# Zero products in TensorE's planned pauses, and a fourth head pair moved by products

## The chip, the cores and the metric

The kernel runs on one core of a Trainium2 chip. The metric is the device time of one execution in microseconds, and a kernel is told by the median of its runs. The time before is 1008.89 us, the median of 3 runs (1008.83 to 1009.3).

## What is computed

```python
# 4 batches, 8 heads, 768 steps, head width 48
for t in range(S):
    state = alpha[:, :, t, :, None] * state + k_t (outer) v_t     # per batch and head
    y[:, :, t] = q_t @ state
x = y as 3072 tokens x 384                                        # fp32
x = ((x @ w_a) * (x @ w_b)) @ w_out            # first network, 384 -> 1536 -> 384
h = x @ w_in
out = (max(h, 0) + alpha2 * min(h, 0)) @ w_out2 # second network, 384 -> 2048 -> 384
```

The weights of both networks arrive as 8-byte floats; q, k, v and alpha are fp32.

## The kernel before

**Chunks and blocks.** The recurrence is cut into 24 chunks of 128 steps of one batch. Four chunks, one of each batch, make a block of 512 tokens, so there are six blocks. A chunk loads its decays (tile La), keys (Lk), queries (Lq) and values (v) over the one DMA queue (SP). VectorE makes the running products of the decays backwards and forwards by two scans (R, L303, and La in place, L313), multiplies the keys by the one (L317) and the queries by the other (L321). TensorE transposes the keys (kps, L360), makes the step-by-step scores (A, L377), the new state (dS, L402), and the output y from the masked scores As (L412) and, from the second block on, from the kept state Z (L422). ScalarE and VectorE split y into a high and a low part (tile x, L464 and L468). Most tiles of a chunk have two buffers (`Ring(2)`): the load of chunk g+2 waits for the last reader of chunk g.

**The fourth pair.** Eight heads of width 48 are four pairs, each padded to two halves of 64 rows. The networks want 384 rows in three groups of 128, so the rows of the fourth pair have to go into the padding of the first three. In block 0 (`start`) TensorE makes the fourth pair first, ScalarE copies it (y3, L449), and a product with a constant 0/1 matrix `shift` adds it to each of the other three (L454). In blocks 1 to 5 six DMAs move the rows inside the tile x (L486).

**Weights.** A unit is 256 columns of one weight matrix; the first network has 18 (a0, b0, o0 to a5, b5, o5), the second 16. `conv` turns a unit of 8-byte floats into a high and a low fp32 part: ScalarE takes the magnitude (L195), VectorE does sign (L203), a clamp from below (L199), main (L208), power (L212) and rest (L216), ScalarE makes the high part (L221), VectorE subtracts it (L224) and adds the rest (L228).

**The networks.** A step of the first network is two up products (pa, pb, nine matmuls each), a copy and a multiplication (a_sb, L627, L630), a split (gh, gl, L526, L530) and, two steps later, nine down matmuls into three accumulators (acc). Each product is three passes (L503, L504, L506). `SEGMENTS` orders the steps: units 0 and 1 for block 0 (four steps), the same for block 1, then units 2 and 3 for either, and so on; then the second network.

**The order of the work.** Nothing is ordered by hand. All operations go into a `Graph` with an engine, a planned duration, a priority (`key`) and their dependences; `Graph.run` plays them through with these durations and writes each engine's instructions in the planned order. At run time each engine works through its own list in that order and waits where it must. Chunks of block 0 have the lowest keys, then the units and chunks by due time. Three PSUM tiles (`ps_mm`) take the up products. Before, `up` takes them by a ring in order of creation (`mring`). `a_sb` has two buffers, handed out by `bring = Ring(2)`.

At the start VectorE clears a tile and TensorE multiplies it eight times (`WARM`, L149).

Of the kernel before, what the change touches and what calls it, by code (L numbers as in the profile page):

```python
# [21 lines left out]
P = 128  # L22
# [9 lines left out]
WARM = 8  # L32
# [6 lines left out]
URGENT = 40000  # L39


class Op:
    __slots__ = ("eng", "dur", "fn", "key", "lat", "need", "users", "soft", "ready", "end", "n")


class Graph:
# [3 lines left out]
    def __init__(self):  # L50
        self.ops = []

    def add(self, eng, dur, fn, key, deps=(), lat=0, after=()):
        o = Op()
        o.eng, o.dur, o.fn, o.key, o.lat = eng, dur, fn, key, lat
        o.users, o.soft, o.ready, o.end, o.need, o.n = [], [], 0, None, 0, len(self.ops)
        for d in {x for x in deps if x is not None}:
            d.users.append(o)
            o.need += 1
        for d in {x for x in after if x is not None}:  # L60
            d.soft.append(o)
            o.need += 1
        self.ops.append(o)
        return o

    def run(self):
        free, ready = {}, {}
        for o in self.ops:
            free.setdefault(o.eng, 0)
            ready.setdefault(o.eng, [])  # L70
            if not o.need:
                ready[o.eng].append(o)
        for _ in range(len(self.ops)):
            best = None
            for e, l in ready.items():
                if l:
                    t = max(free[e], min(o.ready for o in l))
                    if best is None or t < best[0]:
                        best = (t, min((o for o in l if o.ready <= t), key=lambda o: (o.key, o.n)))
# [12 lines left out]

# [19 lines left out]
def body(tc, akq, v, w_a, w_b, w_o1, w_in, w_o2, beta, out):  # L112
# [13 lines left out]
    with ExitStack() as ctx:  # L126
# [31 lines left out]
        )  # L158

        shift = wpool.tile([P, KT, P], F32, name="shift", tag="s1")  # L160
# [8 lines left out]
        G = Graph()  # L169
# [12 lines left out]
        cring = Ring(2)  # L182

        def conv(src, tag, name, key, wait, sink, early=15000):
# [7 lines left out]
            def magnitude():  # L192
                b["c1"] = cpool.tile([P, UC], F32, name="c1", tag="c1")
                b["c2"] = cpool.tile([P, UC], F32, name="c2", tag="c2")
                nc.scalar.activation(out=b["c1"], in_=b["raw"].bitcast(F32)[:, 1::2], func=ACTF.Abs,  # L195
                                     scale=65536.0)

            def floor():
                nc.vector.tensor_scalar(out=b["c1"], in0=b["c1"], scalar1=2.0, scalar2=None,  # L199
                                        op0=ALU.max)  # L200
# [33 lines left out]
            y = G.add("DVE", 550, sign, key, [m])  # L234
            x = G.add("DVE", 550, floor, key, [m, y])
# [7 lines left out]
            return ld, x  # L243

# [4 lines left out]
        for u in range(NU1):  # L249
            for nm, src in (("a", w_a), ("b", w_b), ("o", w_o1)):  # L250
                x = nm, u
                slot_of[x] = len(slot_of)
                uses[x] = []

                def sink(r, x=x):
                    units[x] = as_unit(r, 2 if x[0] == "o" else KT)

                _, done[x] = conv(src[u], f"w{slot_of[x]}", f"{nm}{u}", due[x] - 20000, (), sink)
# [6 lines left out]
        before = {"scan": None, "y3": None}  # L265
# [3 lines left out]
        def chunk(g):  # L269
            s = st[g]  # L270
            n, c = divmod(g, BC)
            start, end = n == 0, n == NB - 1
# [7 lines left out]
            def load(nm, lo, hi):  # L280
                def f():
                    s[nm] = tp.tile([P, hi - lo], F32, name=f"L{nm}", tag=f"L{nm}")
                    nc.sync.dma_start(s[nm], akq[g, :, lo:hi])
                return f
# [5 lines left out]
            kT = lambda: s["k"].rearrange("p (j t) -> p j t", j=NJ)  # L290
            qT = lambda: s["q"].rearrange("p (j t) -> p j t", j=NJ)
            rings = {nm: lrings[nm] for nm in "akq"}
            w = {nm: rings[nm].take() for nm in "akq"}
            use = {nm: rings[nm].use for nm in "akq"}
            la = A("SP", 800, load("a", 0, NA), w["a"], 14000, 2500)
            lk = A("SP", 800, load("k", NA, NA + NC), w["k"], 13900, 2500, [la])
            lq = A("SP", 800, load("q", NA + NC, NA + 2 * NC), w["q"], 13800, 2500, [la])
            lv = A("SP", 800, load_v, vring.take(), 12000, 2500)


            def scan_r():
                s["R"] = tp.tile([P, NJ, CH + 1], F32, name="R", tag="R")
                nc.vector.tensor_tensor_scan(  # L303
                    out=s["R"].rearrange("p j t -> p (j t)")[:, ::-1], data0=s["a"][:, NA - 1 : 0 : -1],
# [3 lines left out]
            def recip():  # L308
                nc.vector.reciprocal(invs[:, :, 0:1], s["R"][:, :, 0:1])

            def scan_a():
                a = s["a"][:, 0 : NA - 1]
# [3 lines left out]
            def mul_k():  # L316
                nc.vector.tensor_tensor(out=kT(), in0=kT(), in1=s["R"][:, :, 1 : CH + 1], op=ALU.mult)  # L317

            def mul_q():
                a = s["a"][:, 0 : NA - 1].rearrange("p (j t) -> p j t", j=NJ)[:, :, 1:]  # L320
                nc.vector.tensor_tensor(out=qT(), in0=qT(), in1=a, op=ALU.mult)  # L321

            r = A("DVE", 1250, scan_r, [la, *rring.take()])
# [4 lines left out]
            rring.use(k1, rc)  # L328
            use["a"](q1)
# [3 lines left out]
            if not start:  # L333
                def decayed():
                    z = Z[:, c, :, :]
                    nc.vector.tensor_tensor(out=z, in0=z, in1=s["R"][:, :, 0:1].to_broadcast([P, NJ, D]),
# [19 lines left out]
            if not end:  # L356
# [13 lines left out]
                use["k"](x)  # L370
# [18 lines left out]
            use["k"](pa)  # L389
# [24 lines left out]

            def pe_y():
                s["y"] = ps_tile("y")
                for j in (KT,) if start else range(NJ):
                    intra(j, start or j == 0, start)
                for j in () if start else range(NJ):
                    for i in range(2):  # L420
                        ps = slice(64 * i, 64 * i + D)
                        nc.tensor.matmul(s["y"][ps, j, :], Z[ps, c, j, :], qT()[ps, j, :],  # L422
                                         start=False, stop=j == NJ - 1)

            py = A("PE", 300 if start else 1600, pe_y, [a0, a1, lv, q1, zs, *aring.take()])
            yhold = aring.last()
            use["q"](pa, py)
# [16 lines left out]
            nt = KT if start else NJ  # L444
            x = py
            if start:
                def ev_3():
                    s["y3"] = wpool.tile([P, CH], F32, name="y3", tag="s0")
                    nc.scalar.copy(s["y3"], s["y"][:, KT, :])  # L449

                def pe_m():
                    for t in range(KT):
                        intra(t, True, False)
                        nc.tensor.matmul(s["y"][:, t, :], shift[:, t, :], s["y3"], start=False, stop=True)  # L454

                x = A("ACT", 280, ev_3, [py, before["y3"]])
                x = before["y3"] = A("PE", 1400, pe_m, [x])
            sring.use(x)
            vring.use(x)
# [15 lines left out]
            s["xh"] = A("ACT", 620, split_h, [x, *w], after=[st[n * BC]["xh"]] if c else ())  # L475
# [3 lines left out]
            if c < BC - 1 or start:  # L479
# [12 lines left out]
        lrings = {nm: Ring(2) for nm in "akq"}  # L492
# [4 lines left out]
        mring, gring, bring, accring, ering = Ring(3), Ring(3), Ring(2), Ring(1), Ring(2)  # L497
# [10 lines left out]
        def up(key, deps, x, w, o):  # L508
# [10 lines left out]
            op = G.add("PE", 9 * MM, f, key, [*deps, *mring.take()])  # L519
            uses[w].append(op)  # L520
            return op, mring.last(), b
# [230 lines left out]
def layout(q, k, v, alpha, moe_w_a, moe_w_b, moe_w_out, moe2_w_in, moe2_w_out, moe2_alpha):  # L752
# [6 lines left out]
    def padded(x, fill):  # L759
# [11 lines left out]

    KT, GR = H * D // P, 64 - D
# [6 lines left out]
        akq=akq, v=vv, w_a=up_units(moe_w_a, rows), w_b=up_units(moe_w_b, rows),  # L779
# [23 lines left out]
```

## Time and profile before

| | us |
|---|---|
| median of 3 runs | 1008.89 |
| profiled execution, its own time | 1011.72 |
| its span, first to last instruction | 1010.0 |
| TensorE busy (matmul) | 978.9 (97% of the span) |
| VectorE busy | 629.6 (62%) |
| ScalarE busy | 249.3 (25%) |
| mean granted TensorE clock | 0.965 |

PE is TensorE (PEld its weight loads), DVE VectorE, ACT ScalarE, POOL GpSimd, SP the DMA queue's engine. A granted clock of 1.00 is 2.4 GHz and 0.50 is 1.2 GHz. L412 is line 412 of the kernel before. A name with an arrow is output and input by the program's tile names.

### The profile page before, as it was taken

What the parts mean: (1) busy time and instruction counts of PE and PEld (TensorE: products, weight loads), DVE (VectorE), ACT (ScalarE), POOL (GpSimd) and SP (SyncE); (2) the same over time, 40 slices, a digit from 0 to 9 for tenths busy, and PEclk for the clock granted to TensorE, in tenths of its full rate; (3) what the DMA queues carried; (4) which work ended last, traced back from release to release, by engine and by line L of the source; (5) the groups of instructions that cost most, each with busy time, mean ns of one, the idle gap of its engine ahead of it and who ended that gap; (6) DMA issues with size and microseconds to landing.
All of it is one profiled execution on the core that took longest, in us unless ns stands there. A gap on an engine that the chain in (4) does not pass through costs nothing.

```text
span 1010.0 us, 12618 instructions
## 1 busy us (share of the span) xinstructions
PE 978.9 (97%) x5192; PEld 786.6 (78%) x5192; DVE 629.6 (62%) x935; ACT 249.3 (25%) x397; POOL 4.4 (0%) x18
## 2 busy tenths in 40 slices
PE   7878799999999999999999999999999999999998
PEld 4656588887887788778778888888888888888886
DVE  6688788877867896888333226455554555545543
ACT  2223344322333243333212112111111111111211
POOL 1000000000000000000000000000000000000000
PEclk6579799999999999999999999999999999999999
DMA  7782200015445563563216553020020100200000
GB/s 275 274 305 85 58 11 1 11 41 174 161 152 173 186 225 117 191 224 137 67 33 225 189 190 147 1 84 11 1 93 1 63 32 1 94 1 0 32 1 32
DMA packets 34090, 103.52 MB, mean 102 GB/s; under 512 B 3889, under 2 KB 3889, under 8 KB 34033
## 3 DMA queue, kind: packets, MB, share of 16 engines
q1 hardware_dynamic: 34032, 102.71, 29.3%
q8 instruction: 41, 0.67, 0.3%
q14 instruction: 17, 0.13, 0.0%
HBM read 73.99 MB, written 26.74 MB: 100 GB/s over the span
## 4 chain that ended last, share of the span: by engine, by line
PE 95%; DVE 2%; DMA 1%; SPq 1%; ACT 0%; issue 0%; ACTq 0%
PE acc L503 12%; PE acc L506 12%; PE acc L504 11%; PE pi L506 7%; PE pi L503 7%; PE pi L504 7%; PE pb L503 5%; PE pa L503 5%; PE pa L506 5%; PE pb L504 5%; PE pb L506 5%; PE pa L504 5%; PE A L377 3%; PE y L412 3%; PE y L422 2%; PE dS L402 1%
## 5 line engine op out<-in xcount | busy, mean ns | idle before, releaser
L526 ACT CAST gh<-ng 128x512 fp32r<-128x512 f32 x96 | 59.6, 620 | 327.2 <-DVE ng L722 275.0
L718 DVE TENSOR_SCALAR ng<-pi,betaT 128x512 f32<-128x512 f32 x96 | 72.1, 751 | 106.8 <-PE pi L506 105.9
L530 DVE TENSOR_TENSOR gl<-ng,gh 128x512 fp32r<-128x512 f32 x96 | 66.3, 691 | 78.5 <-ACT gh L526 78.5
L506 PE MATMUL acc<-gl,v 128*128 128x512 f32 x288 | 113.5, 394 | 0.0
L504 PE MATMUL acc<-gh,v 128*128 128x512 f32 x288 | 112.9, 392 | 0.0
L503 PE MATMUL pi<-x,v 128*128 128x512 f32 x288 | 112.7, 391 | 0.0
L504 PE MATMUL pi<-x,v 128*128 128x512 f32 x288 | 112.7, 391 | 0.0
L630 DVE TENSOR_TENSOR a_sb<-a_sb,pb 128x512 f32<-128x512 f32 x72 | 49.5, 688 | 99.9 <-PE pb L506 99.6
L503 PE MATMUL acc<-gh,v 128*128 128x512 f32 x288 | 111.7, 388 | 0.0
L503 PE MATMUL acc<-gh,wo 128*128 128x512 f32 x216 | 88.2, 409 | 4.5 <-ACT wo L221 4.5
L503 PE MATMUL pa<-x,wa 128*128 128x512 f32 x216 | 87.4, 405 | 4.5 <-DMA x<-x 3.9
L504 PE MATMUL acc<-gh,wo 128*128 128x512 f32 x216 | 85.9, 398 | 2.5 <-DVE wo L228 2.5
L503 PE MATMUL pb<-x,wb 128*128 128x512 f32 x216 | 87.7, 406 | 0.0
L506 PE MATMUL acc<-gl,wo 128*128 128x512 f32 x216 | 86.2, 399 | 0.0
L504 PE MATMUL pa<-x,wa 128*128 128x512 f32 x216 | 85.5, 396 | 0.0
L504 PE MATMUL pb<-x,wb 128*128 128x512 f32 x216 | 85.4, 395 | 0.0
L506 PE MATMUL pi<-x,v 128*128 128x512 f32 x288 | 81.5, 391 | 0.0
L627 ACT COPY a_sb<-pa 128x512 f32<-128x512 f32 x72 | 42.3, 587 | 154.2 <-PE pa L506 154.1
L526 ACT CAST gh<-a_sb 128x512 fp32r<-128x512 f32 x72 | 44.7, 621 | 120.5 <-DVE a_sb L630 117.0
L722 DVE SCALAR_TENSOR_TENSOR ng<-pi,ng 128x512 f32<-128x512 f32 x96 | 66.3, 691 | 3.1
L504 PEld LDWEIGHTS acc<-gh,v 128*128 128x128 f32 x288 | 54.0, 188 | 12.6
L503 PEld LDWEIGHTS acc<-gh,v 128*128 128x128 f32 x288 | 54.1, 188 | 12.1
(93 smaller groups left out, 1469.3 us busy)
## 6 DMA issues: line engine op xcount, KB each, us to landing
w2d<-ws SPq DMA_DIRECT2D x16, 768.0 KB, 3.5
v<-w2d SPq DMA_DIRECT2D x16, 768.0 KB, 5.3
x2d<-x SPq DMA_DIRECT2D x18, 512.0 KB, 3.6
x<-x2d SPq DMA_DIRECT2D x6, 1536.0 KB, 7.1
La<-in_akq SPq DMA_DIRECT2D x24, 258.5 KB, 3.5
Lk<-in_akq SPq DMA_DIRECT2D x24, 256.0 KB, 2.7
Lq<-in_akq SPq DMA_DIRECT2D x24, 256.0 KB, 2.7
v<-in_v SPq DMA_DIRECT2D x24, 256.0 KB, 2.9
```

The source lines that it names most:

```text
L377: nc.tensor.matmul(s["A"][i][:, j, :], kT()[ps, j, :], qT()[ps, j, :], start=True, stop=True)
L412: nc.tensor.matmul(s["y"][64 * i : 64 * i + 64, j, :], s["v"][:, 2 * j + i, :], s["As", i][:, j, :], start=first, stop=last)
L422: nc.tensor.matmul(s["y"][ps, j, :], Z[ps, c, j, :], qT()[ps, j, :], start=False, stop=j == NJ - 1)
L503: nc.tensor.matmul(o, lh, rh, start=first and n == 0, stop=False)
L504: nc.tensor.matmul(o, ll, rh, start=False, stop=False)
L506: nc.tensor.matmul(o, lh, rl, start=False, stop=last and n == len(pairs) - 1)
L526: nc.scalar.copy(gq[idx][0], src())
L530: nc.vector.tensor_tensor(out=gl, in0=src(), in1=gh.bitcast(F32), op=ALU.subtract)
L627: nc.scalar.copy(b["a"], ba["t"])
L630: nc.vector.tensor_tensor(out=b["a"], in0=b["a"], in1=bb["t"], op=ALU.mult)
L718: nc.vector.tensor_scalar(out=b["n"], in0=bh["t"], scalar1=0.0, scalar2=betaT[:, i : i + 1], op0=ALU.min, op1=ALU.mult)
L722: nc.vector.scalar_tensor_tensor(out=b["n"], in0=bh["t"], scalar=0.0, in1=b["n"], op0=ALU.max, op1=ALU.add)
```

## The change

Six edits, made together.

- The eight products at the start go. `Graph.run` calls `fill` wherever its plan shows TensorE without work for over 500 ns (`PAUSE`); `fill` writes products of zeros (bf16, 256 columns) for 70% of that pause at 110 ns each, if one of the three PSUM tiles is free by then. They read the zeros of `ones`.
- The PSUM tiles of `up` are handed out in planned order by a `Pool(3)`, which `fill` and the new products for weights share.
- Block 0: the values of the fourth pair arrive a second time, laid out in the padding rows (`vg`, 192 KB a chunk), so that six products write them in place; the copy y3 and the products with `shift` go. Block 1 (`moved`): the way of block 0 before is used, with the state's part: fourth pair, copy, then the other three and three products with `shift`; its six DMAs go. Blocks 2 to 5 keep the DMAs. The copy y3 takes a buffer of `a_sb` and its turn in `bring`.
- Units a0, b0 and o0 (`on_pe`): subtraction and addition are done by TensorE, as two times three fp32 products (with `ident`, `minus`, `ident`) of 384 columns, and copied out by ScalarE.
- No clamp (L199) in any unit.
- La and R become one tile `ra`, Lk and Lq one tile `kq` with one load of 512 KB, and the two multiplications one (`mul`), which waits for both scans.

```diff
+PAUSE = 500
...
+    def start(self, o):
+        t = o.pool.free() if o.pool else 0
+        return None if t is None else max(o.ready, t)
...
+            if o.eng == "PE" and t - free["PE"] > PAUSE:
+                self.fill(free["PE"], t)
+            if o.pool:
+                o.pool.log.append(o.hold)
...
+class Pool:
+    def __init__(self, n):
+        self.n, self.log = n, []
+    def free(self):
+        ends = [u.end for u in self.log[-self.n]] if len(self.log) >= self.n else []
+        return None if None in ends else max(ends, default=0) + HOP
...
-        warm = wpool.tile([P, MB], BF16, name="warm", tag=f"w{3 * NU1 - 1}")
-        nc.vector.memset(warm, 0.0)
-        wp = ps_mm.tile([P, MB], F32, name="wp", tag="mm")
-        for _ in range(WARM):
-            nc.tensor.matmul(wp, warm[:, 0:P], warm, start=True, stop=True)
+        warm = ones.bitcast(BF16)[:, 0, 2 : 2 + 2 * CH]
+        def fill(t0, t1):
+            t = mpool.free()
+            if t is None or t > t0 + 100:
+                return
+            mpool.log.append([])
+            wp = ps_mm.tile([P, MB // 2], F32, name="wp", tag="mm")
+            for _ in range(int((t1 - t0) * 0.7) // 110):
+                nc.tensor.matmul(wp, warm[:, 0:P], warm, start=True, stop=True)
...
+        cring, mpool, bring = Ring(2), Pool(3), Ring(2)
...
-            x = G.add("DVE", 550, floor, key, [m, y])
...
+            if on_pe:
+                return ld, conv_pe(b, key, x, sink)
...
+        def conv_pe(b, key, x, sink):
+            last = None
+            for n in range(2):
+                cs = slice(n * UC // 2, (n + 1) * UC // 2)
+                p = {}
+                def add(p=p, cs=cs):
+                    p["t"] = ps_mm.tile([P, MB], F32, name="cl", tag="mm")
+                    o = p["t"][:, 0 : UC // 2]
+                    nc.tensor.matmul(o, ident, b["c1"][:, cs], start=True, stop=False)
+                    nc.tensor.matmul(o, minus, b["r"].bitcast(F32)[:, 0:UC][:, cs], start=False, stop=False)
+                    nc.tensor.matmul(o, ident, b["c2"][:, cs], start=False, stop=True)
...
+                m = G.add("PE", 1950, add, key, [x], pool=mpool)
+                last = G.add("ACT", 500, low, key, [m], after=[last])
...
+                if start:
+                    s["vg"] = wpool.tile([P, KT, 2, 64], F32, name="vg", tag=f"s{c % 2}")
+                    nc.sync.dma_start(s["vg"], vg[c])
...
-            k1 = A("DVE", 680, mul_k, [lk, r])
             sa = before["scan"] = A("DVE", 1250, scan_a, [rc])
-            q1 = A("DVE", 700, mul_q, [lq, sa])
+            k1 = q1 = A("DVE", 1220, mul, [lq, sa])
...
+                if start:
+                    for j in range(KT):
+                        intra(j, j == 0, False)
+                    for j in range(KT):
+                        for i in range(2):
+                            nc.tensor.matmul(s["y"][64 * i : 64 * i + 64, j, :], s["vg"][:, j, i, :],
+                                             s["As", i][:, KT, :], start=False, stop=j == KT - 1)
+                    return
+                if moved:
+                    intra(KT, True, False)
+                    inter(KT, True)
+                    return
...
+                def pe_m():
+                    for j in range(KT):
+                        intra(j, j == 0, False)
+                    for j in range(KT):
+                        inter(j, False)
+                    for j in range(KT):
+                        nc.tensor.matmul(s["y"][:, j, :], shift[:, j, :], s["y3"], start=False,
+                                         stop=j == KT - 1)
+                x = A("ACT", 280, ev_3, [py, *bring.take()])
+                py = A("PE", 1900, pe_m, [x])
+                bring.use(py)
+            lring.use(pa, py)
...
-            if c < BC - 1 or start:
+            if c < BC - 1 or start or moved:
                 return
...
-        mring, gring, bring, accring, ering = Ring(3), Ring(3), Ring(2), Ring(1), Ring(2)
+        gring, accring, ering = Ring(3), Ring(1), Ring(2)
...
-            op = G.add("PE", 9 * MM, f, key, [*deps, *mring.take()])
+            op = G.add("PE", 9 * MM, f, key, deps, pool=mpool)
```

`intra(j)` is the two products of pair j's values and masked scores, `inter(j)` the two of its queries and kept state. The line that takes `bring` for a step of the first network stays as it was: `ca = G.add("ACT", 590, copy_a, at[k] - URGENT, [pa, *bring.take()])`; the chunks are created before the steps.

## Rows read from the trace of the kernel before

**Rows 1.** The page's second part: busy tenths and clock in 40 slices of the span.

```profile
PE   7878799999999999999999999999999999999998
PEclk6579799999999999999999999999999999999999
```

**Rows 2.** Windows: stretch, its length, busy us (instructions) by engine, clock, DMA share, GB/s.

```profile
8.70:53.20 44.50, 40.04 (x242) 27.95 (x243) 29.27 (x45) 10.38 (x21) 0.00 (x0) 0.50 0.78 287
...
67.30:76.80 9.50, 6.34 (x16) 4.76 (x17) 9.50 (x14) 3.24 (x5) 0.00 (x0) 0.50 0.58 235
...
101.20:107.30 6.10, 4.79 (x23) 4.02 (x24) 5.53 (x10) 0.91 (x1) 0.00 (x0) 0.50 0.31 86
...
117.80:124.70 6.90, 6.38 (x15) 5.02 (x16) 4.58 (x8) 1.42 (x2) 0.00 (x0) 0.51 0.00 1
...
sum 132.00, PE 105.90 PEld 76.87 DVE 101.47 ACT 37.75 POOL 4.35; mean PE 11.77 PEld 8.54 DVE 11.27 ACT 4.19 POOL 0.48
```

**Rows 3.** Timeline of TensorE at the start: start, us, instruction, idle before and releaser.

```profile
1.26 3.59 PE L149 MATMUL wp<-warm 128*128 128x512 bf16 x8 [1.26 <-DVE warm L146]
5.91 0.63 PE L360 MATMUL kps<-ident,Lk 128*128 128x128 f32 x4 [1.06 <-DVE Lk L317]
9.07 1.10 PE L402 MATMUL dS<-v,ks 128*64 128x48 f32 x16 [2.54 <-DMA v<-in_v]
```

**Rows 4.** The chain that ended last, 22 to 62 us: start, us, what.

```profile
24.45 0.62 PE y L412 x4
25.08 0.73 PE y L454 x2
...
52.70 0.57 PE kps L360 x4
53.27 0.23 PE pa L503
...
55.34 1.09 PE A L377 x16
...
58.70 0.60 PE dS L402 x16
59.30 0.89 PE y L412 x16
60.19 1.01 PE y L422 x16
```

**Rows 5.** Waits of TensorE before 130 us: us in total, times, longest.

```profile
PE acc L503 <- ACT wo L221: 4.5, 1, 4.5
PE pa L503 <- DMA x<-x: 3.9, 3, 2.9
```

**Rows 6.** The same chain, 63 to 69 us, where it runs over VectorE.

```profile
65.53 0.60 DVE gl L530
...
67.00 0.47 DVE c L212
67.47 1.14 DVE R L303
68.61 0.85 DVE c L224
```

**Rows 7.** The same chain: y of block 1's third chunk; its rows moved.

```profile
96.94 1.03 PE y L422 x16
...
112.61 0.76 SPq L486
...
115.97 2.31 DMA x<-x
```

**Rows 8.** Windows of 3.7 to 113 us, and of 94 to 96 us.

```profile
3.70:113.00 109.30, 88.36 (x615) 64.39 (x613) 84.74 (x130) 28.37 (x48) 1.51 (x5) 0.72 0.62 220
...
94.00:96.00 2.00, 0.75 (x18) 0.70 (x20) 2.00 (x5) 0.00 (x0) 0.00 (x0) 1.00 0.41 112
```

**Rows 9.** Waits of the DMA queue before 113 us: us in total, times, longest.

```profile
SPq L283 <- PE y L422: 18.5, 4, 5.7
```

More of the change, by code (lines that the diff above doesn't have):

```diff
@@ L39, with __init__, add @@
 URGENT = 40000
+PAUSE = 500
 class Op:
-    __slots__ = ("eng", "dur", "fn", "key", "lat", "need", "users", "soft", "ready", "end", "n")
+    __slots__ = ("eng", "dur", "fn", "key", "lat", "need", "users", "soft", "ready", "end", "n", "pool", "hold")
 class Graph:
-    def __init__(self):
-        self.ops = []
-    def add(self, eng, dur, fn, key, deps=(), lat=0, after=()):
+    def __init__(self, fill):
+        self.ops, self.fill = [], fill
+    def add(self, eng, dur, fn, key, deps=(), lat=0, after=(), pool=None):
         o = Op()
+        o.pool, o.hold = pool, []
         o.eng, o.dur, o.fn, o.key, o.lat = eng, dur, fn, key, lat
@@ L75, in run @@
             for e, l in ready.items():
-                if l:
-                    t = max(free[e], min(o.ready for o in l))
+                able = [(t, o) for o in l if (t := self.start(o)) is not None]
+                if able:
+                    t = max(free[e], min(x[0] for x in able))
                     if best is None or t < best[0]:
-                        best = (t, min((o for o in l if o.ready <= t), key=lambda o: (o.key, o.n)))
+                        best = (t, min((o for x, o in able if x <= t), key=lambda o: (o.key, o.n)))
             assert best is not None, "the operations wait for each other"
@@ L158, in body @@
         )
-        shift = wpool.tile([P, KT, P], F32, name="shift", tag="s1")
+        minus = const.tile([P, P], F32, name="minus")
+        nc.gpsimd.tensor_scalar(out=minus, in0=ident, scalar1=-1.0, scalar2=None, op0=ALU.mult)
+        shift = gpool.tile([P, KT, P], F32, name="shift", tag="x2")
         nc.gpsimd.memset(shift, 0.0)
@@ L167, in body @@
                 )
-        G = Graph()
+        G = Graph(fill)
         units, uses = {}, {}
@@ L179, in body, with conv @@
             block_at.setdefault(n, at[k])
-        cring = Ring(2)
-        def conv(src, tag, name, key, wait, sink, early=15000):
+        cring, mpool, bring = Ring(2), Pool(3), Ring(2)
+        def conv(src, tag, name, key, wait, sink, early=15000, on_pe=False):
             b = {}
@@ L243, in conv, with low @@
             return ld, x
+        def conv_pe(b, key, x, sink):
[9 more added lines that the diff above has]
+                    nc.tensor.matmul(o, ident, b["c2"][:, cs], start=False, stop=True)
+                def low(p=p, cs=cs, n=n):
+                    nc.scalar.copy(b["r"][:, UC : 2 * UC][:, cs], p["t"][:, 0 : UC // 2])
+                    if n:
+                        sink(b["r"])
+                m = G.add("PE", 1950, add, key, [x], pool=mpool)
+                last = G.add("ACT", 500, low, key, [m], after=[last])
+                m.hold.append(last)
+                cring.use(m)
+            return last
         def as_unit(r, n):
@@ L271, in chunk @@
             n, c = divmod(g, BC)
-            start, end = n == 0, n == NB - 1
+            start, moved, end = n == 0, n == 1, n == NB - 1
             key = block_at[n] - (BC - c) * 7500 - 6000 if n else c * 1000 - 100000
@@ L413, in intra, with inter @@
                                      s["As", i][:, j, :], start=first, stop=last)
+            def inter(j, last):
+                for i in range(2):
+                    ps = slice(64 * i, 64 * i + D)
+                    nc.tensor.matmul(s["y"][ps, j, :], Z[ps, c, j, :], qT()[ps, j, :],
+                                     start=False, stop=last)
             def pe_y():
                 s["y"] = ps_tile("y")
-                for j in (KT,) if start else range(NJ):
-                    intra(j, start or j == 0, start)
@@ L419, in pe_y @@
[L419 to L425, printed above, removed]
-            yhold = aring.last()
-            use["q"](pa, py)
+                if start:
+                    for j in range(KT):
+                        intra(j, j == 0, False)
+                    for j in range(KT):
+                        for i in range(2):
+                            nc.tensor.matmul(s["y"][64 * i : 64 * i + 64, j, :], s["vg"][:, j, i, :],
+                                             s["As", i][:, KT, :], start=False, stop=j == KT - 1)
+                    return
@@ new lines, in pe_y, with ev_3 @@
+                if moved:
+                    intra(KT, True, False)
+                    inter(KT, True)
+                    return
+                for j in range(NJ):
+                    intra(j, j == 0, False)
+                for j in range(NJ):
+                    inter(j, j == NJ - 1)
+            py = A("PE", 1350 if start else 500 if moved else 1600, pe_y, [a0, a1, lv, q1, zs, *aring.take()])
+            yhold = aring.last()
+            if moved:
+                def ev_3():
+                    s["y3"] = gpool.tile([P, CH], F32, name="y3", tag="a_sb")
+                    nc.scalar.copy(s["y3"], s["y"][:, KT, :])
+                def pe_m():
+                    for j in range(KT):
+                        intra(j, j == 0, False)
+                    for j in range(KT):
[6 more added lines that the diff above has]
+                bring.use(py)
@@ L440, in chunk @@
                 state[c] = [x]
[L444 to L459, printed above, removed]
+            nt = KT if start or moved else NJ
+            sring.use(py)
+            vring.use(py)
             def split_h():
@@ L517, in f @@
                              for k in range(KT)], True, True)
[L519 removed]
+            op = G.add("PE", 9 * MM, f, key, deps, pool=mpool)
             uses[w].append(op)
[L521 removed]
+            return op, op.hold, b
         def gsplit(idx, key, deps, src):
```

75 lines of the change are left out of this document (34 added, 41 removed).

## Prediction

> **What bounds the kernel now.** I read the page's slices first, then windows over the uneven part, then TensorE's timeline, its waits and the chain, and last VectorE and the DMA queue there. TensorE is the bound: busy nearly all the time at the full clock from slice 6 on [rows 1]. After 125 us it waits for nothing, so no engine made faster there gives anything back. What can be won lies in the first 125 us, in two forms.
>
> Idle: of the first 132 us TensorE is busy 105.9 [rows 2], which leaves 26.1. The largest pieces are the wait for unit o0 (4.5 us, VectorE working through its list in front of it), and the wait for the rows that DMAs move into block 1's x (3.9) [rows 5].
>
> A low clock: in four stretches the granted clock is 0.50, which is 1.2 GHz. Their busy times of 40.04, 6.34, 4.79 and 6.38 us [rows 2] would take half at 2.4 GHz: 20.0 + 3.2 + 2.4 + 3.1 = 28.7 us lost. The first is all of block 0, in which TensorE works through four chunks with few waits and stays at the low level until some up products have run. The reader should see in rows 3 how it came to that. The eight products of zeros run at 0.43 us each, the low rate; the transposes behind them take 0.63 for four, against 0.57 at the full clock and 1.1 at the low [rows 3, 4]. So zeros do raise the clock. Then TensorE has nothing for 2.54 us and dS, after it, runs at the low rate.
>
> With the eight products themselves (3.6 us), 26.1 + 28.7 + 3.6 = 58.4 us are not useful work. The span is 1010.0 us in an execution of 1011.72, 2.8 us above the median; I take the difference that the change makes and put it on the median.
>
> **Part by part.** *TensorE's own work.* Block 0: a chunk's y now takes four pairs of products (0.62 each at the low clock) and three with `shift` (0.73) [rows 4], 4.67, or 2.3 at the full clock. The new way is six pairs; a pair at the full clock is 0.89 / 4 to 1.01 / 4, say 0.25, so 1.5. Four chunks save 3.3 us. Block 1: three products with `shift` more per chunk, 3 x 0.73 / 2 = 1.1, so 4.4 us more.
>
> The products for a0, b0 and o0 are 18, fp32, of 384 columns, and none like them is in the trace. The nearest of the same type is `shift`'s, 0.37 us at the full clock for 128 columns. That bounds them from below, if columns cost nothing more (6.6 us for 18), and three times it, 1.1, from above (19.7). A product of 512 columns in one pass takes 0.23 [rows 4], so columns alone cannot bring it to the upper end; I take 0.7, together 12.6 us. The Trainium skill (FP8 and Floating Point Precision, TensorE Precision Notes) says that a true fp32 product goes through the array four times; by that estimate one costs 4 x 384/512 x 0.23 = 0.69 and the sum would be 12.4. No product of this size in the trace shows it.
>
> TensorE's useful work grows by 12.6 + 4.4 - 3.3 = 13.7 us. This is the price; whatever the change wins has to come from the 58.4.
>
> *Order.* Here I see a new wait. The copy y3 of block 1 takes its turn in `bring`, and chunks are created before the network's steps. With two buffers, step 0's copy of pa waits for the last product of block 1's third chunk, and step 1's for that of the fourth. Before, the first steps ran before and between these chunks. Now TensorE can make pa0, pb0 and pa1 and then has no PSUM tile free: the remaining steps of block 0, o0's products on TensorE and every `fill` (all take from the same three) stand behind that chunk. Call the time when it is done t6. After t6 there is a backlog (18 us of block 0's steps, the fourth chunk), and block 1's x comes ready within it, since its six DMAs (0.6 us each to issue and 2.31 for the last to land [rows 7]) are gone. So I take TensorE as full from t6 on, as it is now from 125 us on, and what is lost is t6 less the useful work done by then.
>
> That work: block 0 at 0.57 + 0.60 + 1.09 + 1.5 = 3.8 a chunk, 15.0; three chunks of block 1 at 0.57 + 1.09 + 0.60 + 0.89 + 1.01 + 1.1 = 5.3, 15.8; three up products of nine at 0.23, 6.2; a0's and b0's products 8.4. Together 45.4 us.
>
> *t6 by VectorE.* Its busy time from 3.7 to 113 us is 84.7 [rows 8]. That list held, beyond what t6 now needs: the fourth chunk of block 1 (two scans of 1.14, five operations at 0.60, three short ones, about 5.9), the multiplication and split of four steps (8 x 0.60 = 4.8), eight clamps at the 0.47 of L212, which has their shape (3.8), subtraction and addition of three units (6 x 0.86 = 5.2), unit o1 (4.4 without the clamp: two of 0.47, four of 0.86), the parts of a2 and b2 (3.7) and perhaps b1 (4.4; its buffers wait for o0) [rows 6]. That leaves 52 to 57. In that stretch VectorE was busy 84.74 / 109.30 = 78%. I take 81%, as block 0's chunks no longer wait for a slow TensorE: 54.5 / 0.81 + 3.7 = 71 us. The ends: 86% and the short list, 64; 70% and the long one, 85.
>
> *Other bounds on t6.* TensorE: first transposes at about 8.6, since `mul` now waits for both scans and the first fill stands in front of them (the plan's durations put `mul`'s end at 7.9 us, so 50 products; some 16 at 0.21, half of rows 3's 0.43, until the clock rises, the rest at 0.11: 7 us), and 45.4 of work, 54: below 71, so this is not the limit while the clock is high. The buffers: a load of queries already waits for the chunk two before it (18.5 us in four waits [rows 9]); the merged load waits for the last product of y too. Load, multiplication, scores, mask and two parts of y make some 13 to 16 us for each pair of chunks, and y of chunk 0 is done at about 14.5 (8.6 + 0.57 + 1.09, masks behind chunk 1's multiplication 2.0, y 1.5, waits between them), so 14.5 + 3 x 16 = 63. Below 71 as well, but near it. By the same steps y of chunk 2 ends near 29, and x of block 0, with chunk 3 and its split behind it on VectorE, is whole at about 33.
>
> *The clamp, elsewhere.* It goes from all 34 units; behind 125 us TensorE's work hides that, and it counts nothing. If that cover were gone, it would be worth 26 x 0.47 = 12 us of VectorE. The merged multiplication costs what the two cost. The extra 192 KB loads are four and lie before the raw weights; the queue waited 18.5 us for buffers in any case, so I put them at nothing.
>
> Sum: 1008.9 - 58.4 + 13.7 + (71 - 45.4) = 989.8, so 990 us. Every us of t6 is a us of the result.
>
> **The rivals.** *The clock falls again.* `fill` writes nothing while the three PSUM tiles are held, and TensorE waits between block 1's chunks. For it: the clock fell after the waits ahead of 67 and 101 us [rows 2]. Against: between 94 and 96 us TensorE, in the middle of a chunk, waited for over half of the time and the clock stayed at 1.00 [rows 8]. Three chunks at 1.2 GHz would need 31.5 us instead of 15.8 behind an x of block 0 at about 33 us, with the products and ups of 14.6: t6 near 80, so 999 us. The same comes out if the fills are too thin to hold the clock through block 0 and its x is done at 42. The Trainium skill (TensorE: Matmul & The Clock Gate, A second HAM failure mode: psum-queue depth-cycling) says that idling between groups while PSUM buffers are cycled makes the clock fall and rise over and over; by that rule it is this rival's 999 us, and the trace agrees at 67 us and not at 94.
>
> *Slower: the shared ring.* If the wait for `bring` starves TensorE for longer than I think, so that the third chunk of block 1 ends late, all of it shows: past t6 = 90 (45.4 + 58.4 - 13.7) the result is slower than before. Today that chunk's y ends at 98 us [rows 7], behind work that is now shorter or moved back, so t6 must barely improve for this. At 95 it would be 1014.
>
> *Earlier.* The buffers alone set the pace and VectorE packs at over 86%: t6 of 62 and less, 981 or below.
>
> *The zeros do nothing* (the change doesn't do what it says): already the first rival's time; rows 3 speak against it.
>
> **How the numbers follow.** The forecast (t6 of 64 to 78, 983 to 997) has 0.62; the first rival, 997 to 1006, 0.17; the slower one 0.13; the early one 0.06; no change 0.02. About 2 us (0.2%) is what a measurement here can tell from none. Faster 0.85, same 0.02, slower 0.13. The range must leave out no more than 0.2: from 979, the early rival's upper half with the products at their low end (2 us less), to 1006, the end of the first rival, which leaves out the slower case and half the early one.
>
> **What would show it.** Right: granted clock near 1.00 through most of 8 to 35 us; the first up product at about 33; then a stretch in which only attention of block 1 runs on TensorE, with the copy of pa0 waiting; six products with `ident` and `minus` per unit near 0.7 each; no idle after some 75 us; no moves for block 1. Wrong: a clock of 0.50 between 40 and 70, idle on TensorE after 80, fills that run while VectorE's or ScalarE's results for TensorE already lie ready, or t6 far from 71.

## The result, and the profile after

The changed kernel takes 996.53 us, the median of 4 runs (994.34 to 1000.1), against 1008.89 before. The ratio is 0.988 (95% interval 0.985 to 0.991), 12.4 us or 1.2% faster. In a later series it was 0.987 (0.984 to 0.989). The forecast was 990 in a range of 979 to 1006: the change wins as forecast, and 6.5 us of the gain that it counted on didn't come. With 996.53 the median stands at the upper end of the 983 to 997 us that the forecast's own mechanism was given; the profiled execution took 1000.1, which lies among the 997 to 1006 of the first rival (the clock falls again).

The profiled execution has a span of 998.4 us and is the slowest of the four; another profiled one, of the later series, has a span of 994.0 and is called the second below. First the slices of the page, to be held against [rows 1]:

```profile
PE   6979999999999999999999999999999999999997
PEclk9978999999999999999999999999999999999999
```

TensorE is full two slices earlier and its clock is high in the first two. A high clock ahead of the first recorded change is not proof, though: the record begins at 1.00 whatever the rate is. The durations tell more. TensorE's timeline after, from the start to the first up product and then around 75 and 95 us:

```profile
8.94 1.09 PE L414 MATMUL kps<-ident,kq 128*128 128x128 f32 x4 [8.94 <-DVE invs L368]
9.96 2.08 PE L431 MATMUL A<-kq 48*128 48x128 f32 x16
...
13.90 1.27 PE L178 MATMUL wp<-ones 128*128 128x256 bf16 x5
...
16.80 1.16 PE L431 MATMUL A<-kq 48*128 48x128 f32 x16
...
21.38 3.01 PE L178 MATMUL wp<-ones 128*128 128x256 bf16 x26
24.23 0.60 PE L414 MATMUL kps<-ident,kq 128*128 128x128 f32 x4
...
27.67 0.81 PE L287 MATMUL cl<-c,ident 128*128 128x384 f32 x2
28.31 0.81 PE L288 MATMUL cl<-wa,minus 128*128 128x384 f32 x2
28.96 0.81 PE L289 MATMUL cl<-c,ident 128*128 128x384 f32 x2
...
41.36 0.47 PE L576 MATMUL pa<-x,wa 128*128 128x512 f32 x1
...
73.38 1.65 PE L507 MATMUL y<-y,shift 128*128 128x128 f32 x6
74.82 1.49 PE L287 MATMUL cl<-c,ident 128*128 128x384 f32 x2
...
88.63 0.67 PE L455 MATMUL dS<-v,ks 128*64 128x48 f32 x16 [0.78 <-DVE As L438]
90.10 0.44 PE L465 MATMUL y<-As,v 128*64 128x128 f32 x4 [0.79 <-DVE As L438]
...
91.28 1.55 PE L465 MATMUL y<-As,v 128*64 128x128 f32 x12 [0.36 <-ACT y L499]
```

The scores of a chunk take 2.08 us at 9.96 and 1.16 at 16.80, so the clock rises between. There is no fill ahead of the first transposes. The first up product comes at 41.36 us. Products for a unit follow each other at 0.65 us. The third chunk of block 1 is done at 74.8 us, and only behind it come the second half of o0's products and the later steps. The stretch before is the weak one, as windows of it show (columns as in [rows 2]):

```profile
3.70:74.80 71.10, 60.27 (x564) 45.89 (x565) 61.66 (x86) 20.67 (x37) 2.76 (x7) 0.90 0.85 327
...
56.00:60.00 4.00, 3.07 (x34) 2.31 (x36) 4.00 (x7) 0.27 (x1) 0.00 (x0) 0.57 0.92 364
...
64.00:68.00 4.00, 1.26 (x19) 1.03 (x18) 3.85 (x7) 1.53 (x3) 0.00 (x0) 0.85 0.37 141
68.00:72.00 4.00, 3.63 (x38) 2.55 (x40) 4.00 (x6) 0.88 (x2) 0.00 (x0) 0.50 0.00 0
...
92.00:96.00 4.00, 4.00 (x27) 3.26 (x24) 2.20 (x4) 0.06 (x1) 0.00 (x0) 0.50 0.16 24
```

The clock is mostly at 1.2 GHz from 57 us on. From 64 to 68 us TensorE works 1.26 of 4 us while VectorE is busy for 3.85; behind that the clock is at 1.2 GHz again, and once more from 92. ScalarE's timeline shows why TensorE has nothing else to do:

```profile
50.39 0.48 ACT L292 CAST wo<-cl 128x384 fp32r<-128x384 f32 x1 [1.86 <-PE cl L289]
...
72.20 0.57 ACT L700 COPY a_sb<-pa 128x512 f32<-128x512 f32 x1
```

pa0 was ready at 43.6 us, and its copy runs 28 us later: the plan put it behind the third chunk of block 1. pa0 and pb0 hold two of the three PSUM tiles all that time. The third, that of half of o0's products, is copied out at 50.39 us and then free, but the plan hands the tiles out in turn, and the next in turn is pa0's. At run time the copy no longer waits for that chunk's last product, which is done at 74.8; it stands in ScalarE's list behind the chunk's copy y3. TensorE's waits before 130 us, against [rows 5]:

```profile
PE kps L414 <- DVE invs L368: 8.9, 1, 8.9
PE dS L455 <- DVE As L438: 4.2, 3, 2.0
PE y L465 <- ACT y L499: 1.1, 3, 0.4
```

The waits for unit o0 and for moved rows are gone. What is left is the start, and chunks waiting for VectorE with nothing beside them.

### The profile page after: what moved, and what is told of

It reads as the page before. It is cut to its first block, busy times and chain, and to the rows that moved or that the text cites. A ratio compares the mean times of both kernels' runs of the same rounds, so it can differ in the third digit from the quotient of the medians.

```text
span 998.4 us, 12774 instructions
## 1 busy us (share of the span) xinstructions
PE 976.8 (98%) x5309; PEld 790.5 (79%) x5309; DVE 607.2 (61%) x870; ACT 249.3 (25%) x403; POOL 5.7 (1%) x19
## 4 chain that ended last, share of the span: by engine, by line
PE 97%; DVE 1%; DMA 1%; ACT 0%; issue 0%; DVEq 0%; ACTq 0%
PE acc L576 12%; PE acc L577 12%; PE acc L579 11%; PE pi L577 7%; PE pi L579 7%; PE pi L576 7%; PE pb L576 5%; PE pa L576 5%; PE pb L577 5%; PE pb L579 5%; PE pa L577 5%; PE pa L579 5%; PE y L465 3%; PE A L431 3%; PE y L471 2%; PE dS L455 1%
## 5 line engine op out<-in xcount | busy, mean ns | idle before, releaser
L576 PE MATMUL pa<-x,wa 128*128 128x512 f32 x216 | 86.2, 399 | 0.0
L576 PE MATMUL acc<-gh,wo 128*128 128x512 f32 x216 | 85.9, 398 | 0.0
L577 PE MATMUL acc<-gh,wo 128*128 128x512 f32 x216 | 84.6, 392 | 0.0
L577 PE MATMUL pa<-x,wa 128*128 128x512 f32 x216 | 84.6, 392 | 0.0
L576 PEld LDWEIGHTS acc<-gh,v 128*128 128x128 f32 x288 | 54.1, 188 | 12.7
L579 PEld LDWEIGHTS acc<-gl,v 128*128 128x128 f32 x288 | 54.1, 188 | 12.1
```

Of the source, the lines that this page charges most:

```text
L576: nc.tensor.matmul(o, lh, rh, start=first and n == 0, stop=False)
L577: nc.tensor.matmul(o, ll, rh, start=False, stop=False)
L579: nc.tensor.matmul(o, lh, rl, start=False, stop=last and n == len(pairs) - 1)
```

## Experiments

Ratios are to the kernel before on the same chip, each with its 95% interval. They go by the means of the executions; all times below are medians. The runs belong to three series on three chips (rows 1 to 4, 5 to 8 and 9 to 12 of the table), so across series the ratios are the ones to compare.

| kernel | us | ratio | interval |
|---|---|---|---|
| changed, again | 995.83 | 0.987 | 0.984 to 0.989 |
| without zeros | 996.41 | 0.986 | 0.984 to 0.988 |
| low parts by VectorE | 999.81 | 0.989 | 0.987 to 0.991 |
| own buffers for y3 | 987.92 | 0.977 | 0.975 to 0.978 |
| block 1 by DMAs | 987.45 | 0.977 | 0.976 to 0.979 |
| one operation more per unit | 1002.06 | 0.992 | 0.991 to 0.994 |
| own buffers, no zeros | 986.19 | 0.976 | 0.975 to 0.978 |
| own buffers, low parts by VectorE | 986.90 | 0.977 | 0.976 to 0.978 |
| before, block 0's products alone | 1002.94 | 0.994 | 0.993 to 0.995 |
| before, no clamp alone | 1006.74 | 0.997 | 0.996 to 0.998 |
| changed, three edits out | 992.61 | 0.983 | 0.981 to 0.985 |
| the same, first pause filled | 992.39 | 0.983 | 0.981 to 0.985 |

The theory was the prediction's: VectorE sets the time t6 of block 1's third chunk, the shared ring makes TensorE starve until then, zeros hold the clock. The rivals: the zeros do nothing; the ring costs nothing, as VectorE is the bound in any case; TensorE is the one that is late.

**The changed kernel again.**

> The changed kernel again, as the base for the runs beside it: 994 to 1000 us, its third chunk of block 1 done on TensorE at about 75 us.

It was so: 995.83 us, the chunk done at 74.7 in the second profiled execution. There the clock is back at 1.00 when the chunk is done and doesn't fall behind 88 us, and its span is 4.4 us shorter than the first's. In both, TensorE waits 1.9 us in three pieces between 86 and 92 us; in one of the two executions 1.2 GHz follows. The six executions stand in two groups, four at 994.8 to 996.0 and two at 1001.3 and 1002.8; the trace is of one of the first group.

**Without the products of zeros.**

```diff
-PAUSE = 500
+PAUSE = 10**9
```

> The changed kernel without the products of zeros, all else as it is. Theory: they are what holds the clock high in block 0. Without them TensorE runs chunks 0 to 2 at 1.2 GHz, some 7 us of work more, part of which lies in pauses that they fill now: 3 to 8 us slower than the changed kernel, the clock at 0.50 until a0's products at about 28 us. Rival: the fp32 products for units raise the clock anyway and VectorE sets the pace: within 1 us of the changed kernel.

The rival held: 996.41 us, no difference. TensorE's timeline without zeros:

```profile
16.34 1.16 PE L431 MATMUL A<-kq 48*128 48x128 f32 x16
...
23.65 1.11 PE L414 MATMUL kps<-ident,kq 128*128 128x128 f32 x4 [3.25 <-DVE kq L377]
...
42.44 0.47 PE L576 MATMUL pa<-x,wa 128*128 128x512 f32 x1
```

The clock rises at the same place (scores at 1.16 us), with no zero multiplied so far. After a wait of 3.25 us, which zeros filled, it is down until a0's products. That costs 0.8 to 1.1 us at the first up product. So the zeros do hold the clock there, and it is worth next to nothing: the third chunk's transposes wait for VectorE's multiplied keys and start at 23.65 us without zeros and at 24.23 with them.

**Low parts of a0, b0, o0 by VectorE.** Edit: `on_pe=False`.

> The changed kernel with the low parts of a0, b0 and o0 made by VectorE again. Theory (VectorE sets the third chunk of block 1): VectorE gets 5.2 us more before that chunk, TensorE loses 11.7 us of work of which 10 lay before it: 2 to 5 us slower. Rival (TensorE was the one that was late, as the first up product waits behind b0's products from 37 to 41 us): 4 to 8 us faster.

999.81 us: 4.0 more than the changed kernel by the medians, 2.3 by the ratios, whose intervals overlap for the most part. So the times don't show that it is slower. The trace shows the theory's wait: the third chunk ends at 80.6 us. TensorE's timeline shows the place:

```profile
48.17 1.50 PE L507 MATMUL y<-y,shift 128*128 128x128 f32 x6
58.41 1.09 PE L414 MATMUL kps<-ident,kq 128*128 128x128 f32 x4 [8.74 <-issue]
...
80.39 0.48 PE L576 MATMUL pb<-x,wb 128*128 128x512 f32 x1
```

It waits 8.74 us for the second chunk's multiplied keys (VectorE has four low-part operations of o0 and a1 between), with its PSUM tiles held. But the order is another too: pa0 and pa1 come first here, at 35.7 and 37.9 us, and pb0 behind the third chunk. VectorE's time and the order aren't parted in this run.

**Own buffers for y3.**

```diff
-                    s["y3"] = gpool.tile([P, CH], F32, name="y3", tag="a_sb")
+                    s["y3"] = wpool.tile([P, CH], F32, name="y3", tag=f"s{c % 2}")
...
-                x = A("ACT", 280, ev_3, [py, *bring.take()])
+                x = A("ACT", 280, ev_3, [py, *yring.take()])
...
-            op = G.add("PE", 9 * MM, f, key, deps, pool=mpool)
+            op = G.add("PE", 9 * MM, f, key, deps, after=[chain.get("up")], pool=mpool)
+            chain["up"] = op
```

The link between up products is needed: with own buffers and without it, the plan comes to a state in which operations wait for each other over the three PSUM tiles. The link alone, in the changed kernel, leaves the planned order of every engine as it is.

> The changed kernel with two buffers of its own for the copy y3, so that step 0 and 1 of the first network no longer wait for block 1's third and fourth chunk; the up products are kept in their present order by a link from each to the next, which alone changes no order on TensorE. Theory: the wait starves TensorE from 53 to 75 us (some 6 us idle and 7 us lost at 1.2 GHz): 5 to 10 us faster, clock near 1.00 from 41 us on. Rival: VectorE sets the pace there in any case, and the steps only take its time from the chunks: within 2 us of the changed kernel.

987.92 us, 7.9 less than the changed kernel, of the same series and clear of its interval. Windows of it:

```profile
41.00:53.00 12.00, 12.00 (x95) 8.27 (x95) 10.96 (x17) 5.23 (x10) 0.00 (x0) 1.00 1.02 405
53.00:64.00 11.00, 11.00 (x67) 8.19 (x61) 9.00 (x15) 4.50 (x8) 0.00 (x0) 1.00 0.80 295
64.00:75.00 11.00, 11.00 (x87) 8.42 (x87) 8.12 (x13) 2.88 (x5) 0.00 (x0) 1.00 0.29 93
```

TensorE is full and the clock high throughout, with no product of zeros in this stretch, though the third chunk ends later, at 84.5 us: VectorE serves steps in between. So t6 was never the thing by itself. It mattered because the ring tied everything else to it.

**Block 1 by DMAs.**

```diff
-            start, moved, end = n == 0, n == 1, n == NB - 1
+            start, moved, end = n == 0, False, n == NB - 1
```

> The changed kernel with block 1's fourth pair moved by six DMAs again, as before, and so without the copy y3 in the ring of a_sb (up products linked in order). Theory (the shared ring is what costs, the products for the moves little): TensorE saves 4.4 us of products and is not starved, but waits about 6 us for the moved rows unless other steps cover it: 986 to 992 us, faster than the changed kernel. Rival (the products for block 1 are what wins): 1000 us and more.

987.45 us, as good as own buffers, as the theory had it. The up products are linked here as well. TensorE's waits before 130 us sum to 0.5 us behind the start, but that doesn't mean that other steps cover the moved rows. What stands in front of block 1's first up product is this:

```profile
93.14 4.98 PE L178 MATMUL wp<-ones 128*128 128x256 bf16 x44
97.87 0.48 PE L576 MATMUL pa<-x,wa 128*128 128x512 f32 x1
```

The steps of block 0 are done by then, and 44 products of zeros fill the wait. So the moved rows still cost about 5 us. With own buffers 18 zeros (2.13 us) stand at this place, and the products that move the rows take 3.1 us more (four chunks at 0.77). The two ways come out even: moving block 1's rows by products gains nothing over the DMAs, and costs nothing either.

**One operation more per unit.**

```diff
+            def floor():
+                nc.vector.tensor_scalar(out=b["c1"], in0=b["c1"], scalar1=0.0, scalar2=None,
+                                        op0=ALU.max)
```

> The changed kernel with one more VectorE operation per unit, a clamp at zero, which alters no value. Theory (VectorE sets when the third chunk of block 1 is done, six to eight clamps of 0.47 us lie before it): 2 to 4 us slower than the changed kernel. Rival (the buffers' round of load, products and masks sets it): within 1 us.

1002.06 us, 6.2 more by the medians and 5.4 by the ratios. The size is more than expected and the reason another, as TensorE's timeline shows:

```profile
71.90 1.60 PE L512 MATMUL y<-y,shift 128*128 128x128 f32 x6
73.34 0.81 PE L292 MATMUL cl<-c,ident 128*128 128x384 f32 x2
...
76.92 0.69 PE L581 MATMUL pb<-x,wb 128*128 128x512 f32 x1
```

The third chunk is not later (73.3 us). With longer planned units the plan put pb0 behind that chunk (first product at 76.92 instead of 44.97 us) and all of o0's products too, 4.0 us of TensorE's work that no longer lay before it. So most of the price of an edit on VectorE came here through the order, not through VectorE's time.

**Own buffers, no zeros; own buffers, low parts by VectorE.** Edits: `PAUSE = 10**9`; `on_pe=False`.

> Own buffers for y3 as in the run before, and no products of zeros. Theory: once TensorE has work, the 90 products of zeros (0.11 us each, 10 us) are load, the clock holds without them: 1 to 5 us faster than with them, 983 to 987. Rival (zeros hold the clock in block 0): 1 to 5 us slower, 989 to 993.

986.19 us. By the ratios (0.976 and 0.977, on two chips) it can't be told from own buffers with zeros: neither the theory's gain nor the rival's loss is shown.

> Own buffers for y3, and the low parts of a0, b0 and o0 by VectorE again. Theory: with own buffers TensorE is full from 10 us on, so 11.7 us of products less show in part: 980 to 986. Rival (VectorE's 5.2 us more make units a0 and b0 late and TensorE waits for them): 989 to 994.

986.90 us, between the two expectations and not to be told from own buffers: 11.7 us of TensorE's products are saved, and nothing of it shows. The trace has it as zeros: 195 products of zeros in it against 90 with `on_pe`, some 11.5 us more of them at 0.11 each. TensorE's work went and waits came, which the zeros fill.

**The kernel before with block 0's products alone.** The `vg` edits on the kernel before.

> The kernel before with only block 0's fourth pair made in place by products with the values laid out a second time (no copy y3, no products with the 0/1 matrix). Theory (the round trip over ScalarE and the low clock of block 0 go together: without it TensorE works through a chunk without waits and the clock rises by itself, as it did without zeros in the changed kernel): first up product at 33 to 40 us instead of 48.5, 5 to 10 us faster than before. Rival (the clock stays at 1.2 GHz in block 0 for another reason): the products save 4 x 1.7 us of low-clock work, 0 to 4 us faster.

1002.94 us, 6.6 less than before, half of what the whole change gives. TensorE's timeline:

```profile
17.69 2.08 PE L372 MATMUL A<-Lq,Lk 48*128 48x128 f32 x16
...
25.17 1.16 PE L372 MATMUL A<-Lq,Lk 48*128 48x128 f32 x16 [0.51 <-PE dS L397]
...
38.97 0.50 PE L494 MATMUL pa<-x,wa 128*128 128x512 f32 x1 [1.30 <-ACT wa L213]
```

The first up product comes at 38.97 us instead of 48.5. The clock rises between 17.7 and 25.2 us, and no longer stays low to the end of block 0. But what made TensorE work faster is not quite what the expectation said: it still has waits of 0.5 to 3 us in block 0, and the clock falls and rises twice more by 48 us. And in the kernel before TensorE was busy all of the 8 us from 24 to 32, at a granted 0.50, so waits alone don't tell the two apart. The 6.6 us are the shorter work and the higher clock together; no run parts them.

**The kernel before without the clamp alone.** The clamp out, the scale of the magnitude 2^-112.

> The kernel before with only the clamp taken out of every unit. Theory (in the changed kernel one operation of VectorE per unit was worth 5.5 us, and unit o0 was waited for): 2 to 5 us faster than before. Rival (in the kernel before TensorE at its low clock is the bound of block 0, and the clamps lie beside it): within 1 us.

1006.74 us, 2.8 less, inside the theory's 2 to 5. Whether it comes by VectorE's time or, as above, by another order isn't shown.

**Three edits out.** The edit of block 1 by DMAs, with `PAUSE = 10**9` and `on_pe=False`; then the same with one fill, at time 0:

```diff
-            t = mpool.free()
-            if t is None or t > t0 + 100:
+            if t0 > 0:
                 return
```

> The changed kernel without three of its edits: block 1 moved by DMAs again, low parts by VectorE again, no products of zeros; what stays is block 0's products, no clamp, merged loads, PSUM tiles in planned order. Theory (the gain is theirs, the other three give nothing or cost): 982 to 988 us. Rival: over 996 us, if the three that go were needed.

992.61 us: by the ratios 3.8 us less than the changed kernel, with intervals that just touch, and not the 982 to 988 of the theory. The four edits that stay give 17 us on the kernel before. Windows of it, and under them of own buffers with low parts by VectorE:

```profile
75.00:88.00 13.00, 10.85 (x77) 8.46 (x74) 10.80 (x18) 2.98 (x5) 0.00 (x0) 0.61 0.27 81
88.00:98.00 10.00, 5.32 (x71) 4.12 (x69) 8.20 (x12) 4.04 (x7) 0.00 (x0) 0.95 0.28 91
```

```profile
75.00:88.00 13.00, 13.00 (x125) 10.15 (x125) 12.47 (x19) 5.79 (x10) 0.00 (x0) 1.00 0.34 113
88.00:98.00 10.00, 10.00 (x108) 8.02 (x105) 9.06 (x14) 3.37 (x6) 0.00 (x0) 1.00 0.24 80
```

Without all three the clock falls in the pauses of block 1's chunks, and TensorE stands still for 5.1 us in front of block 1's first up product (at 99.19 us), where the moved rows arrive; the run below, the same there, has this wait as one of 5.38 us for the DMAs of x. In the run shown under it there is neither. Own buffers without zeros hold the clock from 75 to 98 us too, at 1.00. The runs that beat this one miss none or one of the three; which of them is missed most was not run.

> The run before with one fill, in the first pause of TensorE (50 products of zeros before the first transposes), which the changed kernel doesn't make, as its rule wants a PSUM tile free earlier than the plan gives one at time 0. Theory (zeros raise the clock, so the first two chunks run at 2.4 GHz, but VectorE and the loads set the pace of block 0): clock high from about 6 us, first transposes at the full rate, and 0 to 2 us faster than without it. Rival (block 0 is bound by TensorE there): 3 us faster.

992.39 us, no difference. Its timeline:

```profile
1.39 9.19 PE L177 MATMUL wp<-ones 128*128 128x256 bf16 x57 [1.39 <-POOL ones L179]
10.42 0.60 PE L413 MATMUL kps<-ident,kq 128*128 128x128 f32 x4
...
23.07 0.66 PE L413 MATMUL kps<-ident,kq 128*128 128x128 f32 x4 [3.65 <-DVE kq L376]
...
98.89 0.76 PE L575 MATMUL pa<-x,wa 128*128 128x512 f32 x1 [5.38 <-DMA x<-x]
```

The first transposes run at the full rate, so these 57 zeros do raise the clock from a standing start, and at 23 us the third chunk waits for its keys just the same.

## Why the prediction was right, and where it was off

**Right: where the gain can lie.** All of it is in the first 125 us; behind, TensorE waits for nothing in either trace.

**Right: the shared ring.** The new wait that was read from the diff is there, with the copy of pa0 at 72.20 us, and own buffers are worth 7.9 us. The sum took it in through t6: 71 us said, 74.8 and 74.7 measured. That it came so near is in part luck: VectorE was busy 61.66 of 71.10 us by then, 87% instead of 81%, and its list was longer than the 54.5 us said; the two errors went against each other. And "every us of t6 is a us of the result" holds only while the ring is shared: with own buffers t6 is 84.5 and the time 7.9 us less.

**Off: TensorE is full from t6 on.** That step failed. Behind 75 us it waits three more times in either profiled execution (0.78, 0.79, 0.36 us), each time for VectorE or ScalarE in the fourth chunk. In the first the clock is also low from 75 to 77 and from 91 to 97 us, which costs half of some 2.4 and 6 us of work. Together 1.9 + 1.2 + 3.0 = 6.1 us; in the second only the waits are there, 1.9. The backlog that was to cover the fourth chunk couldn't start, since step 1 waits for that chunk in the same ring; the prediction had this in its text and not in its sum. Two of the signs that it named for being wrong came with this: a clock of 0.50 between 40 and 70 us, and idle on TensorE after 80.

**How the sum comes out.** The 6.5 us missing at the median are not these 6.1. In the profiled executions the sum gives a span of 1010.0 - 58.4 + 13.7 + 25.6 = 990.9 us, and 7.5 and 3.1 us more were measured. t6 came 3.8 and 3.7 us late, which the sum counts in full, and the products cost 2.3 us less than they were priced at (below). So 3.8 + 6.1 - 2.3 = 7.6 us for the first, and 3.7 + 1.9 - 2.3 = 3.3 for the second. That is an estimate, as the useful work done before t6 was not counted again.

**Off: x of block 0 at 33 us.** Its last chunk's y is done at 37.0 and its low part at 39.4, and the first up product, at 41.4, stands in TensorE's list behind all of b0's products. Of the useful work assumed before t6, pa1 (2.1 us) didn't come, as half of o0's products (1.9) took the third PSUM tile.

**Off: the first fill.** The prediction had it in front of the first transposes. The plan gives a PSUM tile as free from 250 ns on, `fill` wants it within 100, and nothing is written. The last experiment shows that this cost nothing, there on the kernel with three edits out.

**Sizes.** Unit products held: 0.65 each for 0.7, 11.6 us for 12.6; by this the Trainium skill's four passes (FP8 and Floating Point Precision, TensorE Precision Notes), 0.69, come out near too. The moved rows of block 1 were priced too high, at 1.1 us a chunk and 4.4 in all; at the high clock a chunk's three take 0.77 us in the timeline (51.88 to 52.65), 3.1 in all, and 1.4 us at the low one (73.38 to 74.82).

**The zeros.** The prediction gave the clock of block 0 to them. The run without zeros refutes that for its first rise: the clock rose in the same place. Nor do the eight zeros at the start of the kernel before raise it each time: the transposes behind them took 0.63 us in the trace that the prediction read, and 1.09 in those of the two runs on the kernel before. What ended the low clock of block 0 is in good part the new way of block 0, with which alone it rises ahead of the up products. Why TensorE's clock rises between block 0's first two chunks here, and not until the first up products in the kernel before, isn't settled. The rival of a clock that falls again while PSUM tiles are held came in part: most of 57 to 75 us and the window from 92 to 96 stand at 0.50, with the chunk's end only 4 us late. The rule of the Trainium skill (TensorE: Matmul & The Clock Gate, A second HAM failure mode: psum-queue depth-cycling), that idling between groups while PSUM is cycled makes the clock fall and rise, agrees with this trace in the idling and the falls (2.02 us of waiting ahead of 67.94 us, and 0.50 behind it). That the cycling of PSUM has a part in it no run shows.

**Where the gain came from.** Not all parts were run alone. Alone on the kernel before, block 0's products give 6.6 us and the clamp 2.8. Out of the changed kernel, the zeros are worth nothing, block 1's products with their turn in the ring cost 8.4 by the medians and 9.4 by the ratios, and what the unit products are worth isn't clear of the noise. The kernel with three edits out keeps four and stands 17 us below the one before; block 0's products and the clamp make 9.4 of that, if the two add up. The merged loads, the PSUM tiles in planned order and the start without the eight products, which would have the rest, were not run by themselves. The fastest kernels are four that can't be told apart, at 986 to 988 us: own buffers for y3 (as they are, without zeros, or with low parts by VectorE), and block 1 by DMAs.

## What to carry to other kernels

A buffer lent to a second use brings its queue along: where rings are handed out in order of creation, read who stands in front of whom before counting on overlap. Before filling an engine's pauses to keep its clock, ask what sets the pace there; filling can pay only where the clock is on the path. A busy engine is not a used one once its pauses are filled: look at what it does in front of the next step that waits. When orders come from a planner, change one duration and see whether the order changes, since its effect can be larger than the operation's time.

## What the runs showed that was not expected

The record of TensorE's clock reads 1.00 up to the first change it holds: four transposes at 8.94 us take 1.09 us, the rate of 1.2 GHz, under a recorded 1.00. In the kernel before without the clamp all of block 0 runs so: the scores take 2.08 us at 35.56, and the record is 1.00 from the start to 64 us. Durations have to be read there, and mean granted clocks of executions can't be compared. Fifty-seven products of zeros from 1.39 us on bring the rate up before 10.42 us.

The changed kernel's executions spread from 994.8 to 1002.8 us; of two that were profiled, the slower is the one whose clock fell after the waits near 90 us. Own buffers, with TensorE full, spread by 1.3 us.
